# The first part's order of work with additions to its ranks, a buffer of its own for the second chunk's q, and x in a pool of its own

## The chip, the cores and the metric

The kernel runs on one core of a Trainium2 chip. The core has five engines that run side by side, each working through its own instructions in the order in which they were written: TensorE (PE, matrix products and transposes into PSUM), VectorE (DVE), ScalarE (ACT), GpSimd (POOL, used only for constants at the start) and SyncE (SP, which here does nothing but issue DMA transfers). An instruction waits for semaphores that others raise; while it waits, everything behind it on its engine waits too. The metric is the device time of one execution, in microseconds (us).

## The reference

Pooled attention, then a feed-forward layer with softplus. Cut to what is computed:

```python
# q, k, v: 8 batches x 8 heads x 576 positions x 64
k_p = k.reshape(B, H, 72, 8, D).mean(axis=3)      # 72 pooled keys
v_p = v.reshape(B, H, 72, 8, D).mean(axis=3)
scores = (q @ k_p^T) / sqrt(D);  attn = softmax(scores)
x = (attn @ v_p) as 4608 tokens x 512
h = x @ w_in                                      # 512 x 2048
g = max(h, 0) + log1p(exp(-|h|))                  # softplus
out = g @ w_out                                   # 2048 x 512
```

## The kernel before, in words

The 4608 tokens are cut into 18 chunks of 256 (two tiles of 128). For each chunk the kernel makes the attention (transposes of q, scores, minimum, exponentials, sum, division, transposes of the probabilities, product with the pooled values, which gives x), then the products with w_in, softplus, and the products with w_out. x, the weights and g are each split into a rounded high part and a low rest, and three products (high by high, high by low, low by high) stand for one.

There are two parts, each with an order of its own, which a planner writes. This case is mostly about the first part: chunks 0 to 2 complete, the attention of chunk 3, and, at the same time, the loading and conversion of the weights. The weights come in as 64-bit floats; for each of 16 blocks (128 columns of w_in and 128 rows of w_out) DVE takes six instructions and ACT one to build a 32-bit number and split it (lines 791 to 822: `bits`, `clamp`, `shift`, `sign`, `lowest`, `high` on ACT, `rest`). Chunks 0 to 2 use each block as soon as it is converted, which gives PE work while the next block is converted. The second part (chunks 3 to 17) starts when the first part's products end, at about 200 us of the trace, and uses from chunk 4 on a scheme with fewer products, for which combined weights were made and put to memory (`t_dram`), and are loaded back by `load_sums`.

**The planner** (`Order`). The kernel first lists its operations with `op(engine, cost, fn, after, slots, ...)`: on which engine, how long it is thought to take, which operations it follows, and which buffers ("slots") it takes. An operation's rank is the longest chain of planned costs behind it; `first` is added to it. `run` then goes through time: of the operations that can start on the engine that is next to be ready, within 0.4 us of its earliest start, the one with the highest rank plus `first` is taken. The outcome is the order of the instructions of each engine, and the buffer of each slot:

```python
t, o = max(((t, o) for t, o in could if o.engine == best[1] and t < min(best[0], by)),
           key=lambda x: (x[1].rank + x[1].first - ..., -x[1].i))
```

The planner's times order the work; on the chip each engine follows that order and waits where it must. Operations are numbered as they are listed: 0 to 21 are batch 0 of keys and values, 22 to 39 batch 1, then ten for each of the weight blocks 0 to 10 (40 to 49 for block 0, the first two being loads on SP, and so on), seventeen for each of the blocks 11 to 15, then the attention of chunks 0, 1 and 2, the products of chunks 0 and 1 (five operations for each of 16 blocks), the attention of chunk 3, the products of chunk 2, and the keys of batch 2.

**SP's queue at the start.** All loads are issued by SP, in the planned order. They are: batch 0's two key halves and its leftover rows (`kvst` L867, `kvl` L855), chunk 0's q (L308), the first half of weight block 0 (`wst` L760), chunk 1's q, the second half of block 0 (L757), batch 1's first key half, batch 0's two value halves, batch 1's second key half and leftover rows, chunk 2's q, block 1, chunk 3's q, and so on.

**The buffer of q.** One buffer holds the q of a chunk (tag `A4`). In the first part chunks 1 and 2 use the buffer of chunk 0, so a tile of q is loaded only when PE has transposed the same tile of the chunk before (`q_free`, set by the operation `qT`, L337):

```python
if 0 < c < N1:
    qt_[c] = qt_[0]
...
o_q.append(op(SYNC, 1.4, load,
              [] if c == 0 else [q_free[c - 1, t]] if c < N1 else ...
```

**The staging slots.** Four slots of 4 KB a partition (kind `ld`: tags L, X4, X5, X6) hold the key and value halves and the leftover rows until PE has used them (`kps` L921, `vps` L938, `kvlp` L880), and later the raw blocks 11 to 15 of the weights. Batch 0's values have a place of their own.

**Other buffers.** `spin` rotates the tags of the transposed q (`qT`), of the outputs (`o`) and of a conversion buffer (`wg`) in the order in which the instructions are written. x has two buffers (`X01`, `X23`) in the pool `one`; the minima and sums (`mn`, `sm`) have a pool of two buffers each behind it; `pe` is a tile with 16 floats more than it uses.

## Time and profile before

| | |
|---|---|
| three runs | 916.7, 917.85, 921.63 us; median 917.85 |
| the profiled execution | 915.2 us |
| its span, first to last instruction | 913.5 us |
| mean granted TensorE clock | 0.994 |
| PE, busy with products | 888.3 us, 97% of the span |
| DVE, ACT | 648.7 us (71%), 407.3 us (45%) |
| moved by DMA | 191.12 MB, mean 209 GB/s |

The span is the time from the first to the last instruction of the profiled execution; its own time is 1.7 us longer, and the median of the runs 2.65 us longer still. In the rows of stages that follow, the columns are: the stretch in us, its length, then for PE, PE's weight loads, DVE, ACT and POOL the busy us with the number of instructions, then the granted PE clock (1.00 is full speed), the mean busy share of the 16 DMA engines (which can pass 1, since packets overlap) and GB/s. In rows of a timeline the columns are start and length, both in us, engine, line, operation, the tile written and the tiles read, shapes and count, and in brackets the idle time just before with what ended it. Rows of waits give who waited, for whom, the total in us, how often, and the longest.

### The profile page before, as it was taken

Reading aid. Unit: us, or ns where it says so; the run is one execution under the profiler, and the core shown is the slowest. Engines: PE = TensorE matmul, PEld = TensorE weight load, DVE = VectorE, ACT = ScalarE, POOL = GpSimd, SP = SyncE. Lnnn points to the kernel's source line nnn. Section 1 sums busy time; section 2 is a strip of 40 time slices with the busy share of each in tenths; the row PEclk is TensorE's granted clock in tenths of the full one; section 3 lists DMA queues with packets and bytes.
Section 4 is the critical chain, followed back from the end, with each engine's and each line's share of the span. In section 5 each row is a group of like instructions: output and inputs, shape, how many; then the busy total and the mean of one; then the engine's idle time right before and its main releaser. Section 6 shows DMA issues by size and latency. Waiting matters only on the chain.

```text
span 913.5 us, 20504 instructions
## 1 busy us (share of the span) xinstructions
PE 888.3 (97%) x8304; PEld 842.9 (92%) x8304; DVE 648.7 (71%) x1600; ACT 407.3 (45%) x824; POOL 2.4 (0%) x19
## 2 busy tenths in 40 slices
PE   4899999999999999999999999999999999999997
PEld 2678989888899999999999999999999999999997
DVE  4799988867877767787777755787666565747454
ACT  4765433344354544444353535453535343434332
POOL 1000000000000000000000000000000000000000
PEclk9899999999999999999999999999999999999999
DMA  8974625545789679789868866687656565746572
GB/s 234 265 255 144 211 93 187 153 158 155 261 288 270 215 208 249 222 256 238 236 208 243 245 201 198 215 252 223 222 168 222 192 208 184 230 144 233 161 238 84
DMA packets 107085, 191.12 MB, mean 209 GB/s; under 512 B 46064, under 2 KB 60400, under 8 KB 106992
## 3 DMA queue, kind: packets, MB, share of 16 engines
q1 hardware_dynamic: 106992, 189.82, 68.0%
q8 instruction: 65, 1.06, 0.5%
q14 instruction: 28, 0.23, 0.1%
HBM read 167.25 MB, written 22.54 MB: 208 GB/s over the span
## 4 chain that ended last, share of the span: by engine, by line
PE 94%; DVE 3%; DMA 1%; ACT 0%; issue 0%; SPq 0%; DVEq 0%; ACTq 0%
PE h L494 43%; PE m L684 30%; PE acc L516 7%; PE sc L357 3%; PE acc L576 3%; PE avp L461 2%; PE qTp L337 2%; PE avp L468 1%; PE ptp L420 1%; PE ltp L432 1%; DMA kvst<-in_k_dram 1%; PE kps L921 1%; DMA kvl<-in_v_dram 1%; DVE pm L397 0%; PE kvlp L880 0%
## 5 line engine op out<-in xcount | busy, mean ns | idle before, releaser
L494 PE MATMUL h<-x,w 128*128 128x256 f32 x3456 | 430.2, 279 | 0.7 <-DVE w L822 0.7
L494 PEld LDWEIGHTS h<-x,w 128*128 128x128 f32 x3456 | 414.9, 188 | 4.1 <-DVE w L822 0.9
L543 ACT ACTIVATE g<-h 128x512 f32<-128x512 f32 x120 | 71.8, 598 | 279.3 <-PE h L494 278.7
L684 PE MATMUL m<-w,so 128*128 128x256 f32 x1344 | 172.6, 278 | 0.0
L684 PEld LDWEIGHTS m<-w,so 128*128 128x128 f32 x1344 | 162.6, 188 | 0.0
L684 PE MATMUL m<-w,gh 128*128 128x256 f32 x672 | 131.9, 285 | 0.0
L594 DVE TENSOR_TENSOR sf<-g 128x128 f32<-128x128 f32 x112 | 32.8, 293 | 130.3 <-ACT g L543 129.4
L684 PEld LDWEIGHTS m<-w,gh 128*128 128x128 f32 x672 | 101.9, 188 | 1.9
L608 ACT CAST so<-sf 128x512 fp32r<-128x512 f32 x112 | 69.7, 622 | 55.4 <-DVE sf L597 54.9
L684 PE MATMUL m<-w,gl 128*128 128x256 f32 x336 | 93.7, 279 | 0.0
L613 DVE TENSOR_TENSOR so<-sf,so 128x512 fp32r<-128x512 f32 x112 | 77.4, 691 | 21.9 <-ACT so L608 21.7
L564 DVE TENSOR_TENSOR gl<-g,gh 128x384 fp32r<-128x384 f32 (+1 forms) x120 | 67.3, 561 | 0.6 <-ACT gh L557 0.5
L684 PEld LDWEIGHTS m<-w,gl 128*128 128x128 f32 x336 | 63.1, 188 | 0.0
L516 PE MATMUL acc<-w,g 128*128 128x512 f32 x192 | 60.8, 397 | 0.5 <-ACT g L499 0.5
L557 ACT ACTIVATE gh<-h 128x384 fp32r<-128x384 f32 (+1 forms) x120 | 59.2, 493 | 0.0
L499 ACT ACTIVATE g<-h 128x256 fp32r<-128x256 f32 x96 | 31.7, 382 | 59.0 <-PE h L494 52.8
L705 DVE TENSOR_TENSOR o<-o,m 128x256 f32<-128x256 f32 x98 | 39.7, 418 | 3.4 <-ACT o L697 0.6
L516 PEld LDWEIGHTS acc<-w,g 128*128 128x128 f32 x192 | 33.9, 187 | 6.9 <-ACT g L499 0.7
L364 DVE TENSOR_REDUCE mn<-sc 128x4 f32<-128x288 f32 x72 | 31.2, 452 | 10.6 <-PE sc L357 10.4
L516 PE MATMUL acc<-w,gl 128*128 128x512 f32 x96 | 38.0, 396 | 0.0
L597 DVE TENSOR_TENSOR sf<-g,sf 128x128 f32<-128x128 f32 x112 | 32.7, 292 | 3.9
L406 DVE TENSOR_TENSOR pe<-E,sm 128x96 f32<-128x96 f32 x72 | 15.2, 253 | 25.8 <-PE ltp L432 25.8
(165 smaller groups left out, 930.3 us busy)
## 6 DMA issues: line engine op xcount, KB each, us to landing
w<-wi SPq DMA_DIRECT2D x224, 512.0 KB
out_dram<-o SPq DMA_DIRECT2D x36, 256.0 KB
q<-in_q_dram SPq DMA_DIRECT2D x32, 256.0 KB
wst<-in_moe_w_in_dram SPq DMA_DIRECT2D x32, 256.0 KB
wst<-in_moe_w_out_dram SPq DMA_DIRECT2D x16, 512.0 KB
wi<-w SPq DMA_DIRECT2D x16, 512.0 KB
kst<-in_k_dram SPq DMA_DIRECT2D x24, 288.0 KB
vst<-in_v_dram SPq DMA_DIRECT2D x24, 256.0 KB
```

The source lines that it names most:

```text
L494: nc.tensor.matmul(out=ps[:, 0:CT], lhsT=row(w, kc), rhs=x[:, kc], start=first and kc == j == 0, stop=last and kc == KC - 1 and j == 2)
L499: nc.scalar.activation(out=g, in_=ps[:, 0:CT], func=AF.Softplus)
L516: nc.tensor.matmul(out=accs[c][t], lhsT=a[:, ts], rhs=w, start=f == 0 and j == 0, stop=f == FC - 1 and j == 2)
L543: nc.scalar.activation(out=g, in_=x.rearrange("p (b i) -> p b i", i=P), func=AF.Softplus)
L557: nc.scalar.activation(out=gh, in_=quarters(c, x.rearrange("p (b i) -> p b i", i=P)), func=AF.Softplus)
L564: nc.vector.tensor_tensor(out=gl, in0=quarters(c, g), in1=gh.bitcast(F32), op=ALU.subtract)
L594: tt(out=sf[:, 2], in0=g[:, 0], in1=g[:, 2], op=ALU.add)
L597: tt(out=sf[:, 3], in0=g[:, 3], in1=sf[:, 1], op=ALU.subtract)
L608: nc.scalar.copy(out=so[:, 0], in_=ss[c, u])
L613: nc.vector.tensor_tensor(out=so[:, 1], in0=sf, in1=so[:, 0].bitcast(F32), op=ALU.subtract)
L684: nc.tensor.matmul(out=ms[c][n], lhsT=x, rhs=y, start=u == 0 and j == 0 and n in (1, 6, 5, 4), stop=u == FP - 1 and j == 2 and n in (2, 7, ...
L705: nc.vector.tensor_tensor(out=o, in0=in0, in1=m[n], op=how)
```

## The change

1. Chunk 1's q gets memory of its own: a staging slot of the kind `ld`, taken from its load to its second transpose. Its load follows no other operation. Chunk 2's q goes to chunk 0's buffer and follows chunk 0's transposes; chunk 3's is as before.
2. 110 of the first part's 647 operations get an addition to `first`, from -450 to +1090 (the table `HASTE`), by their number.
3. The planner's idea of the first part is altered: loads of weights, keys and values cost 1.5 in place of 1.75; SP begins at 0.8; the table of the exponential is taken to be loaded already.
4. The rotating tags are replaced by the tags that the planner gave the slot (`qT`, `o`, `wg`, `mn`, `sm`).
5. x gets a pool of its own ahead of `one`, with the minima's 64 bytes ahead of it, so that its address modulo 256 is what it was; the sums get a pool behind `one`; `pe` loses its 16 floats.
6. A buffer is made by whichever of its operations comes first in the order (`if not kp`, `if not vp`).
7. In the second part `load_sums` loses its lead of 500.

The second part's list is otherwise unchanged, but it starts from the first part's ends and buffer names.

```diff
+    mpool = ctx.enter_context(tc.tile_pool(name="mpool", bufs=1))
+    xpool = ctx.enter_context(tc.tile_pool(name="xpool", bufs=1))
     one = ctx.enter_context(tc.tile_pool(name="one", bufs=1))
-    two = ctx.enter_context(tc.tile_pool(name="two", bufs=2))
+    spool = ctx.enter_context(tc.tile_pool(name="spool", bufs=1))
...
-    def spin(tags, shape, dtype, name):
-
-        tags.append(tags.pop(0))
-        return one.tile(shape, dtype, tag=tags[-1], name=name)
...
-            x = one.tile([P, 2, HP, CT], F32R, tag={"a": "X01", "b": "X23"}[name or "ab"[c % N1]],
+            x = xpool.tile([P, 2, HP, CT], F32R, tag={"a": "X01", "b": "X23"}[name or "ab"[c % N1]],
...
-        def qT_out(self, ps):
-            self.q = spin(Q, [P, HP, P], F32, "qT")
+        def qT_out(self, ps, tag):
+            self.q = one.tile([P, HP, P], F32, tag=tag, name="qT")
...
-                self.mn = two.tile([P, 2, HP], F32, tag="mn", name="mn")
+                self.mn = mpool.tile([P, 2, HP], F32, tag="mn" + tag, name="mn")
...
-            pe = one.tile([P, 6 * R + 16], F32, tag="pe", name="pe")
-            self.pe = pe[:, 0:6 * R].rearrange("p (a n r) -> p a n r", a=2, n=3)
+            self.pe = one.tile([P, 2, 3, R], F32, tag="pe", name="pe")
...
+    todo.begin, todo.table = {SYNC: 0.8}, "exp"
...
-            return op(SYNC, 1.75, fn, slots=[stages[0 if early else i]], lag=2.2)
+            return op(SYNC, 1.5, fn, slots=[stages[0 if early else i]], lag=2.2)
...
-        o_k = [op(SYNC, 1.75, load(k, i), slots=[st[i]], lag=2.2) for i in range(2)]
-        o_v = [op(SYNC, 1.75, load(v, i), slots=[vt[i] or vt[0]], lag=2.2) for i in range(2)]
+        o_k = [op(SYNC, 1.5, load(k, i), slots=[st[i]], lag=2.2) for i in range(2)]
+        o_v = [op(SYNC, 1.5, load(v, i), slots=[vt[i] or vt[0]], lag=2.2) for i in range(2)]
...
-        o_q, subs = [], []
+        o_q, subs, s_q1 = [], [], Slot("ld")
         for t in range(T):
             def load(t=t):
-                if 0 < c < N1:
+                if c == 1 and c not in qt_:
+                    qt_[c] = one.tile([P, T, H, D], F32, tag=s_q1.name, name="q")
+                elif c == 2:
                     qt_[c] = qt_[0]
                 elif c not in qt_:
                     new_q(c)
                 load_q_tile(c, t)
             o_q.append(op(SYNC, 1.4, load,
-                          [] if c == 0 else [q_free[c - 1, t]] if c < N1 else
-                          [q_free[c - 1, i] for i in range(T)], lag=2.4))
+                          [] if c < 2 else [q_free[0, t]] if c < N1 else
+                          [q_free[c - 1, i] for i in range(T)], [s_q1] if c == 1 else [], lag=2.4))
...
+    HASTE = {27: -130, 29: -3, 34: -120, 36: -120, 45: 40, 46: 20, 48: -180, 55: -2, 56: -10,
+             57: -450, 58: 20, 62: -10, 64: 200, 72: -4, 73: -10, 77: -50, 82: -20, 93: 80, 94:
...
+             220: 40, 222: 5, 230: 2, 231: 70, 255: -20, 258: -10, 259: 40, 274: -180, 283:
+             1090, 285: -50, 286: 230, 289: -10, 295: -10, 297: 670, 302: 50, 308: -4, 316: -10,
+             321: -50, 322: -3, 325: -440, 330: -100, 352: -3, 361: -120, 362: -6, 368: -330,
...
+             575: -140, 583: 30, 610: -20, 620: 4, 635: -80, 638: -310, 641: 40}
+    for i, x in HASTE.items():
+        todo.ops[i].first += x
     with tc.manual_schedule(engines={ACT, DVE, PE, SYNC}):
         for o in todo.run():
             o.fn()
...
         t_ready.setdefault(u, []).append(
             op(SYNC, 2.0, lambda: load_t(u, part), [*after, made[u, part] if u >= U1 else None],
-               lag=2.4, first=500))
+               lag=2.4))
```

More of the change, by code (lines that the diff above doesn't have):

```diff
@@ L251, in k_pool @@
         def k_pool(i):
-            if i == 0:
+            if not kp:
                 kp.append(one.tile([SP, H, D], F32, tag="kp", name="kp"))
@@ L262, in v_pool @@
         def v_pool(i):
-            if i == 0:
+            if not vp:
                 vp.append(one.tile([P, HP, D], F32, tag="vp", name="vp"))
@@ L375, in less, with exp_sum @@
                     [P, 2, 2, SP]), op=ALU.subtract)
-        def exp_sum(self, j, ps):
+        def exp_sum(self, j, ps, tag):
             if j == 0:
-                self.sm = two.tile([P, H], F32, tag="sm", name="sm")
+                self.sm = spool.tile([P, H], F32, tag="sm" + tag, name="sm")
             for m in range(HP):
@@ L384, in exp_sum, with sum @@
                                      accum_out=self.sm[:, h:h + 1])
-        def sum(self):
-            self.sm = two.tile([P, H], F32, tag="sm", name="sm")
+        def sum(self, tag):
+            self.sm = spool.tile([P, H], F32, tag="sm" + tag, name="sm")
             nc.vector.tensor_reduce(out=self.sm, in_=e_[self.c][:, self.t], axis=AX.X, op=ALU.add)
@@ L517, in ffn2, with copy_out @@
                                  start=f == 0 and j == 0, stop=f == FC - 1 and j == 2)
-    def copy_out(c, t, tag=None):
-        o = one.tile([P, DM], F32, tag=tag, name="o") if tag else spin(O, [P, DM], F32, "o")
+    def copy_out(c, t, tag):
+        o = one.tile([P, DM], F32, tag=tag, name="o")
         if t % 2 == 0:
@@ L788, in bits @@
             else:
-                g = x["g", k] = spin(O, [P, 1, 4 * P], I32, "wg")
+                g = x["g", k] = one.tile([P, 1, 4 * P], I32, tag=gslot[k].name, name="wg")
                 up = x["raw", k].unsqueeze(1).rearrange("p x (n w) -> p x n w", w=2)[:, :, :, 1]
@@ L972, in attend @@
             o = op(PE, 0.5, lambda x=x, s=s_q: x.qT(bank(s, "qTp")),
-                   [o_q[t], *([av[c - 1]] if c == N1 else [])], [s_q])
+                   [o_q[t], *([av[c - 1]] if c == N1 else [])], [s_q, *([s_q1] if c == 1 else [])])
             q_free[c, t] = o
-            o = op(ACT, act(512), lambda x=x, s=s_q: x.qT_out(s.tile), [o], [s_q, s_qT])
+            o = op(ACT, act(512), lambda x=x, s=s_q, n=s_qT: x.qT_out(s.tile, n.name), [o], [s_q, s_qT])
             ends, ss = [], [Slot("bank"), Slot("bank")]
@@ L980, in attend, with exp_sum @@
             for i, s in enumerate(ss):
-                d = op(DVE, 0.46, lambda x=x, i=i, s=s: x.least(i, s.tile), [p, *ends],
+                d = op(DVE, 0.46, lambda x=x, i=i, s=s, n=s_mn: x.least(i, s.tile, n.name), [p, *ends],
                        [s, s_mn])
                 if c < N1:
-                    def exp_sum(x=x, i=i, s=s, e=s_E[0], t=t):
+                    def exp_sum(x=x, i=i, s=s, e=s_E[0], t=t, n=s_sm):
                         if c == 0 and 0 not in e_:
@@ L1005, in attend @@
             if c == N1:
-                ends = [op(DVE, 0.75, x.sum, [ex], [s_sm])]
+                ends = [op(DVE, 0.75, lambda x=x, n=s_sm: x.sum(n.name), [ex], [s_sm])]
             o = op(DVE, 1.45, x.norm, ends, [*s_E, s_sm, s_pm, s_pe])
@@ L1054, in feed, with copy @@
                 h = {}
-                def copy(t=t, h=h):
-                    h["o"] = copy_out(c, t)
+                def copy(t=t, h=h, s=s):
+                    h["o"] = copy_out(c, t, s.name)
                 o = op(DVE if t % 2 else ACT, 0.65, copy, [before2], [s, acc_slots[c][t]])
@@ L1142, in pooled_attention_softplus_ffn @@
     other = [b for b in BANKS if b not in acc_banks]
-    kinds = {"h": other[:2], "acc": other[2:4], "bank": other[4:], "ld": LD, "q": "a", "pT": "a", "qT": "ab", "lt_": "a",
+    kinds = {"h": other[:2], "acc": other[2:4], "bank": other[4:], "ld": LD, "q": "a", "pT": "a", "qT": Q, "lt_": "a",
              "pe": "a", "mn": "ab", "sm": "ab", "E": "a", "kp": "a", "vp": "a", "S": "ab", "x": "b",
@@ L1175, in steady_attention @@
             qT_done[c].append(o)
-            o = op(ACT, act(512), lambda x=x, s=s: x.qT_out(s.tile), [o], [s, s_qT])
+            o = op(ACT, act(512), lambda x=x, s=s, n=s_qT: x.qT_out(s.tile, n.name),
+                   [o], [s, s_qT])
             last, ss = [], [Slot("bank"), Slot("bank")]
@@ L1181, in steady_attention @@
             for i, s in enumerate(ss):
-                last = [op(DVE, 0.46, lambda x=x, i=i, s=s: x.least(i, s.tile), [p, *last],
+                last = [op(DVE, 0.46, lambda x=x, i=i, s=s, n=s_mn: x.least(i, s.tile, n.name), [p, *last],
                            [s, s_mn])]
@@ L1198, in probabilities @@
             s_sm, s_pm, s_pe = Slot("sm"), Slot("G"), Slot("pe")
-            o = op(DVE, 0.76, x.sum, [ex], [s_E, s_sm])
+            o = op(DVE, 0.76, lambda x=x, n=s_sm: x.sum(n.name), [ex], [s_E, s_sm])
             o = op(DVE, 0.38, x.reciprocal, [o], [s_sm])
```

6 lines of the change are left out of this document (3 added, 3 removed), and 7 rows, old and new, of the table HASTE.

## The prediction

> **What bounds the kernel now.** I read the page's totals first, then a table of stages, then the waits of TensorE (PE) and of the DMA queue, and last single instructions of the first 50 us.
>
> ```profile
> PE 888.3 (97%) x8304; PEld 842.9 (92%) x8304; DVE 648.7 (71%) x1600; ACT 407.3 (45%) x824; POOL 2.4 (0%) x19
> ```
>
> PE works 888.3 of the 913.5 us, so no new order of the same work can win more than 25.2 us plus what a low clock costs. Where these lie is seen in the table of stages (busy us of each engine with its instructions, granted clock, DMA share, GB/s):
>
> ```profile
> 0.00:18.00 18.00, 8.15 (x90) 4.15 (x90) 6.03 (x11) 7.74 (x30) 2.37 (x19) 1.00 0.84 200
> 18.00:26.00 8.00, 5.29 (x73) 3.31 (x74) 3.76 (x9) 2.52 (x13) 0.00 (x0) 0.57 1.16 294
> 26.00:35.00 9.00, 7.87 (x68) 5.90 (x68) 7.12 (x15) 6.72 (x32) 0.00 (x0) 1.00 0.73 189
> 35.00:40.00 5.00, 4.05 (x77) 3.16 (x81) 4.33 (x9) 4.81 (x22) 0.00 (x0) 0.66 1.10 317
> 40.00:80.00 40.00, 35.01 (x355) 29.70 (x345) 37.03 (x76) 26.32 (x69) 0.00 (x0) 1.00 0.70 230
> 80.00:140.00 60.00, 60.00 (x386) 54.16 (x387) 55.10 (x82) 22.24 (x52) 0.00 (x0) 1.00 0.50 164
> 140.00:200.00 60.00, 59.46 (x393) 52.63 (x392) 47.64 (x104) 23.56 (x60) 0.00 (x0) 1.00 0.51 157
> 200.00:300.00 100.00, 99.76 (x939) 92.41 (x939) 77.65 (x181) 46.72 (x83) 0.00 (x0) 1.00 0.76 238
> 300.00:900.00 600.00, 600.00 (x5872) 589.02 (x5871) 403.67 (x1099) 264.11 (x467) 0.00 (x0) 1.00 0.71 215
> 900.00:913.50 13.50, 8.69 (x76) 8.49 (x74) 6.37 (x16) 2.60 (x5) 0.00 (x0) 0.97 0.10 39
> ```
>
> PE idles 9.85 us before 18, 2.71 to 26, 1.13 to 35, 0.95 to 40 and 4.99 from 40 to 80; then it is full until 900 (0.8 us missing in all), and the last 13.5 us belong to the second part. So what is won before 80 reaches the end one for one, and behind 80 there is nothing to win. From 40 to 80 VectorE (DVE) is the tighter engine, 37.03 of 40 against PE's 35.01. Who PE waits for between 10 and 80 (us in total, times, longest):
>
> ```profile
> PE ltp L432 <- DVE pe L406: 4.9, 4, 1.5
> PE kps L921 <- DMA kvst<-in_k_dram: 3.7, 1, 3.7
> PE sc L357 <- ACT kT L225: 1.6, 2, 1.4
> PE qTp L337 <- DMA q<-in_q_dram: 1.5, 2, 1.2
> PE h L494 <- DVE w L822: 0.7, 1, 0.7
> ```
>
> Two are loads (5.2 us, both before 21 us), three are the order of DVE's and ScalarE's (ACT's) work (7.2 us, all behind 32 us).
>
> **The change part by part.**
>
> *Chunk 1's q in memory of its own.* Now its load waits for chunk 0's transposes, and everything behind it in SP's queue waits too. SP's timeline (start, length), its wait, the chain's piece for the second batch's keys, and DMA microsecond by microsecond:
>
> ```profile
> 6.15 1.75 SPq L760 DMA_DIRECT2D wst<-in_moe_w_in_dram  x2
> 12.07 1.11 SPq L308 DMA_DIRECT2D q<-in_q_dram  x2
> 13.24 0.88 SPq L757 DMA_DIRECT2D wst<-in_moe_w_out_dram  x1
> 14.16 0.42 SPq L867 DMA_DIRECT2D kvst<-in_k_dram  x1
> 15.79 1.15 SPq L867 DMA_DIRECT2D kvst<-in_k_dram  x1
> ```
> ```profile
> SPq L308 <- PE kT L219: 3.2, 1, 3.2
> ```
> ```profile
> 14.16 6.41 DMA kvst<-in_k_dram
> ```
> ```profile
> 10.00:11.00 1.00, 1.00 (x3) 0.29 (x2) 0.77 (x2) 0.00 (x0) 0.00 (x0) 1.00 0.88 279
> 11.00:12.00 1.00, 1.00 (x7) 0.79 (x7) 0.60 (x1) 0.58 (x1) 0.00 (x0) 1.00 0.02 6
> 12.00:13.00 1.00, 0.79 (x9) 0.55 (x8) 0.00 (x0) 0.92 (x3) 0.00 (x0) 1.00 0.00 0
> 13.00:14.00 1.00, 0.97 (x60) 0.97 (x64) 0.20 (x1) 0.97 (x3) 0.00 (x0) 1.00 0.70 160
> ```
>
> SP issues nothing from 7.90 to 12.07, 4.17 us. Without the wait all issues behind it come 4.17 us sooner: chunk 1's two q transfers at 7.9, w_out of block 0 at about 9.1, the second batch's first keys at 10.0. The transfers themselves gain less, since the DMA engines are busy to 11.0 with what is there already; the hole that is filled is 0.98 + 1.00 + 0.30 = 2.3 us. So keys that land at 20.57 land at about 18.3, and PE's 3.7 us wait for them shrinks by 2.3. Bounds: 0, if another load is put ahead of the keys in the hole, and 4.17, if the keys pass some of what is ahead. I take 2.3. PE's 1.5 us for q (the two waits before 17 us) need no term of their own: they lie ahead of the same keys.
>
> The price is a staging slot. Four exist; batch 0's two key halves and its leftover rows take three, and the fourth, which batch 1's first keys had, may now go to q. Those keys then need one that is given back, when these end:
>
> ```profile
> 5.97 1.08 PE L921 MATMUL kps<-kvst,zm 128*64 128x256 f32 x2 [5.97 <-DVE kvst L914]
> 10.10 1.11 PE L921 MATMUL kps<-kvst,zm 128*64 128x256 f32 x2
> 16.42 0.63 PE L337 MATMUL qTp<-ident,q 128*128 128x128 f32 x4 [0.33 <-DMA q<-in_q_dram]
> ```
>
> The first is free at 7.05, before SP comes to the keys at 10.0: no cost. The second key half, issued at 15.79 now and at 11.6 then, would take the one free at 11.21: no cost. If they were given the slots the other way round, 1.2 us of the 2.3 would go. q's own slot is free at 17.05 or sooner, for the second batch's values, which come later.
>
> *Clock.* While PE waits for these keys its clock falls. Timeline of PE, then the clock (the column after the engines) by microsecond:
>
> ```profile
> 20.70 3.65 PE L921 MATMUL kps<-kvst,zm 128*64 128x256 f32 x8 [3.66 <-DMA kvst<-in_k_dram]
> 35.95 1.11 PE L357 MATMUL sc<-kT,qT 64*64 64x72 f32 x27 [1.37 <-ACT kT L225]
> 42.27 0.39 PE L432 MATMUL ltp<-ident,pe 128*96 128x128 f32 x2 [1.20 <-DVE pe L406]
> 51.01 0.39 PE L432 MATMUL ltp<-ident,pe 128*96 128x128 f32 x2 [1.44 <-DVE pe L406]
> ```
> ```profile
> 18.00:19.00 1.00, 0.00 (x0) 0.00 (x0) 0.00 (x0) 1.00 (x9) 0.00 (x0) 0.76 1.03 354
> ...
> 25.00:26.00 1.00, 1.00 (x53) 0.92 (x46) 0.46 (x1) 0.00 (x0) 0.00 (x0) 0.83 1.32 173
> ...
> 38.00:39.00 1.00, 1.00 (x12) 0.24 (x5) 1.00 (x2) 1.00 (x9) 0.00 (x0) 0.50 1.07 351
> ```
>
> The clock falls in the microsecond from 18 and is back within that from 25; from 20.70 to about 25.3 PE runs at half speed, which costs 2.3 us; from 35.95 to 39.0 again, 1.5 us. With the keys at 18.3 the idle is 1.3 us instead of 3.66. Rows disagree on whether that is short enough: after 1.20 and 1.44 us the clock stayed (it is 1.00 from 40 to 80), after 1.37 us at 35.95 it had fallen. So 0 to 3.8 us, and I take 1.1, half of the first stretch.
>
> The Trainium skill, "TensorE: Matmul & The Clock Gate", Part 1, says that the clock halves after an idle window of about 3.4 us and recovers after one that is busy, and that the windows run free of the kernel. By that no idle of 1.3 us can halve it, and 2.3 would stand where I have 1.1; the fall before 35.95, with no idle there above 1.4 us, speaks against the rule taken alone, so I keep the half.
>
> *The list's corrections.* 110 of the 647 operations of the first part get an addition to their rank. By the planner's costs in the code, ranks run from 0 to about 165 in this stretch, so the entries beyond 100 decide an order wherever two operations of an engine are ready within 0.4 us, and those below 10 settle near ties. No instruction is added. Early entries push batch 1's leftover products (27), second key half (34) and key transposes (36) back by 120 to 130 on PE, draw forward one exponential of chunk 1 (283), its rounded x (297) and its transposed weights (286) on ACT, and push the conversion of weight blocks 0 and 1 back where attention is ready (48, 57). They concern just the 7.2 us of PE's waits for DVE and ACT. Both ends: all 7.2 won, or as much lost again. DVE limits it: it must deliver the same work, and from 40 to 80 it has 40 - 37.03 = 3.0 us to spare. Earlier it idles more (4.2 us from 18 to 26, 1.9 to 35), in part for a transfer that now starts sooner:
>
> ```profile
> DVE wg L791 <- DMA wst<-in_moe_w_out_dram: 2.8, 1, 2.8
> ```
>
> I take 2.5, a little below DVE's 3.0. Behind 80 PE has no idle, so the many later entries are worth 0; cover there is PE's backlog of products, and without it each would cost what it displaces.
>
> *Edits at nothing.* The planner's own costs (1.5 for 1.75, a start at 0.8, the table already there) act through the order alone and are in the 2.5. Fixed tags in place of rotated ones give the planned buffers. Moving x, mn and sm adds no instruction, and x keeps its phase; tiles ahead of pe move by 64 bytes modulo 256, for which no row shows a price: 0. In the second part the load of the combined weights loses its lead of 500; PE misses only 0.24 us from 200 to 300, and the cover is the time from the last of these issues to the products of the block that it serves. The issues' first and last start, and the products of chunk 4, 48 of this kind for eight blocks:
>
> ```profile
> L665 SPq DMA_DIRECT2D w<-t x16: 370/444/857, 222.0 to 259.9; - x16
> ```
> ```profile
> L684 PE MATMUL m<-w,gh x40: 276/280/385, 261.7 to 299.8; 128*128 128x256 f32 x40
> ```
>
> The last block's products come near 299, 39 us after its load at 259.9. I take 0; a load that came later than that would cost what it is late.
>
> *Sum.* 2.3 + 1.1 + 2.5 = 5.9 us. The profiled execution took 915.2 us (913.5 us of span and 1.7 around it), so 909.3; the median of the three runs, 917.85, lies 2.65 above that execution, so the forecast as a median is 912.0.
>
> **The rivals.**
>
> *Corrections that work fully.* Hole 2.3, clock 2.3, and 6 of the 7.2: 10.6 us, 907.3. For it: the waits are in four or five places with neighbours ready. Against: DVE's 3.0 us.
>
> *Hidden by DVE.* Keys come sooner, but DVE sets when the first products can run, and the 2.3 us turn into longer waits for pe and w; only some 1 us stays: 916.9. For it: DVE's 93% from 40 to 80 and the four waits for pe. Against: DVE too starts sooner, since its own 2.8 us wait is behind the same stall.
>
> *Slower: batch 1's keys come too late.* Ranks cut by 120 to 130 hold them back on PE, whose order is fixed once written. Then kT, for which PE waits 1.6 us already, is later than now, chunk 2's scores with it, and the DVE results behind them. Decisive is whether kT is ready later than the 36 us of now; then the waits for kT and pe double (+1.6 + 4.9) with another cold stretch like the second (+1.5), against 2.3 won: +5.7, 923.5. For it: the size of the entries. Against: the work put ahead on PE is ready and short.
>
> *The stall only changes its owner.* q has the slot, and the keys wait for one in its place, as long as q did: 917.9. The slot free at 7.05 speaks against it.
>
> **How the numbers follow.** The forecast has 0.50, working fully 0.16, hidden by DVE 0.20, slower 0.09, changed owner 0.05. The forecast's own range is 908.5 to 915.0 (0 to 2.3 for the clock, 0 to 4 for the ranks and the hole's 1.2 for a slot). A measurement of this kernel can tell about 0.5%, 4.6 us, from no change: faster is below 913.3. Of the forecast's 0.50 about 0.36 lie there, with 0.16 of the first rival 0.52; same has 0.14, 0.20, 0.05 and 0.01, together 0.40; slower 0.08. From 906.5 to 919.0 hold nearly all of the forecast, hidden and changed owner, and half of working fully: about 0.82.
>
> **What would show it.** SP issues chunk 1's q within 0.2 us of the weights before it, and DMA has no empty microsecond between 11 and 14; PE's wait for the keys is about 1.3 us and they land near 18.3; the clock at 20 to 25 is 1.00 or 0.50; PE's waits for pe, kT and w add up to about 4.7; PE is full from about 75 on and the second part begins some 6 us sooner, at 194 instead of 200. The forecast is wrong if DMA has a new hole before the keys, if kT comes later than 36 us, if DVE's idle before 35 stays as it is, or if PE shows idle between 80 and 300.

## The result, and the profile after

The changed kernel takes 905.18 us in the median of four runs (902.67 to 906.46), beside 919.74 us for the kernel before on the same chip: a ratio of 0.9844, 95% interval 0.9813 to 0.9875. In a second set of six runs it was 0.9876 (0.9847 to 0.9906). The forecast was 912.0 with a range of 906.5 to 919.0. The direction is right, but the time lies below the range: the gain is 14.6 us (11.4 by the second ratio), where the sum had 5.9. The profile of the kernel after shows the fastest of these ten executions (902.67 us); the second set has a profile of its own (906.36 us), and where they differ in what is read from them, it is said.

The totals of the kernel after, then its stages in the columns used before:

```profile
PE 884.9 (98%) x8304; PEld 840.5 (93%) x8304; DVE 649.3 (72%) x1600; ACT 407.4 (45%) x824; POOL 2.4 (0%) x19
```
```profile
0.00:18.00 18.00, 8.89 (x93) 4.57 (x94) 8.43 (x15) 8.28 (x37) 2.37 (x19) 1.00 0.82 236
18.00:26.00 8.00, 7.32 (x120) 5.90 (x119) 7.65 (x18) 7.63 (x29) 0.00 (x0) 1.00 1.09 316
26.00:35.00 9.00, 8.52 (x114) 5.61 (x112) 7.43 (x20) 7.79 (x33) 0.00 (x0) 1.00 0.95 268
35.00:40.00 5.00, 4.66 (x49) 4.09 (x48) 4.45 (x11) 4.95 (x25) 0.00 (x0) 1.00 1.05 384
40.00:80.00 40.00, 39.35 (x348) 33.76 (x348) 38.73 (x71) 23.42 (x52) 0.00 (x0) 1.00 0.64 205
...
140.00:200.00 60.00, 60.00 (x460) 53.50 (x459) 49.77 (x109) 24.77 (x58) 0.00 (x0) 1.00 0.48 161
200.00:300.00 100.00, 100.00 (x906) 94.19 (x906) 77.83 (x192) 44.90 (x80) 0.00 (x0) 1.00 0.78 242
```

The span fell from 913.5 to 900.9 us, 12.6. PE's busy time fell by 3.4 (888.3 to 884.9; in this execution no stretch ran at a low clock), its idle time by 9.2. By the rows, idle fell by 0.7 up to 18 us, 2.0 to 26, 0.7 to 35, 0.6 to 40, 4.3 to 80 and 0.8 from 80 to 300. DVE is 2.4 us further on at 18 us (8.43 for 6.03), 6.3 at 26 and 8.4 at 80. PE's largest waits from 10 to 80 us in the kernel after:

```profile
PE qTp L335 <- DMA q<-in_q_dram: 1.7, 1, 1.7
PE kps L918 <- DMA kvst<-in_k_dram: 0.8, 1, 0.8
PE sc L355 <- ACT qT L342: 0.7, 1, 0.7
```

The waits for `pe` (4.9), `kT` (1.6) and the weights (0.7) have all but gone in this execution; in the second profile PE still waits 2.0 us for `pe`. DVE's wait up to 80 us for the scores that PE makes, before and after:

```profile
DVE mn L364 <- PE sc L357: 7.3, 5, 3.0
```
```profile
DVE mn L362 <- PE sc L355: 2.1, 1, 2.1
```

SP's timeline in the kernel after, its wait, and the microsecond in which DMA moves nothing:

```profile
5.99 1.41 SPq L757 DMA_DIRECT2D wst<-in_moe_w_in_dram  x2
7.44 0.47 SPq L754 DMA_DIRECT2D wst<-in_moe_w_out_dram  x1
12.15 0.37 SPq L306 DMA_DIRECT2D q<-in_q_dram  x1
12.56 0.58 SPq L864 DMA_DIRECT2D kvst<-in_k_dram  x1
13.24 1.38 SPq L306 DMA_DIRECT2D q<-in_q_dram  x2
```
```profile
SPq L306 <- PE qTp L335: 5.7, 2, 3.3
```
```profile
12.00:13.00 1.00, 0.85 (x46) 0.74 (x48) 0.00 (x0) 1.00 (x3) 0.00 (x0) 1.00 0.00 0
```

This is not the picture that was forecast. SP still stands still for 4.2 us, from 7.91 to 12.15, and DMA still has its hole. What waits now is the second tile of chunk 2's q (operation 302, with +50), which goes into chunk 0's buffer. What has changed is what stands ahead of the stall: w_out of block 0, at 7.44 instead of 13.24. Batch 1's keys go out at 12.56 instead of 14.16, ahead of chunk 1's q. PE's timeline after shows them in use:

```profile
15.27 0.63 PE L335 MATMUL qTp<-ident,q 128*128 128x128 f32 x4 [1.74 <-DMA q<-in_q_dram]
16.66 1.91 PE L918 MATMUL kps<-kvst,zm 128*64 128x256 f32 x8 [0.76 <-DMA kvst<-in_k_dram]
```

They are worked on at 16.66 instead of 20.70, in 1.91 us instead of 3.65 at half clock. The first products of the kind `acc<-w,gh` on the second part's line start at 192.4 instead of 203.9; from there to the end of the span it is 708.5 us, and 709.6 before. So some 11 us are won in the first part and one behind it.

### The profile page after: what moved, and what is told of

It reads as the page before. It is cut to its first block, busy times and chain, and to the rows that moved or that the text cites. A ratio compares the mean times of both kernels' runs of the same rounds, so it can differ in the third digit from the quotient of the medians.

```text
span 900.9 us, 20496 instructions
## 1 busy us (share of the span) xinstructions
PE 884.9 (98%) x8304; PEld 840.5 (93%) x8304; DVE 649.3 (72%) x1600; ACT 407.4 (45%) x824; POOL 2.4 (0%) x19
## 4 chain that ended last, share of the span: by engine, by line
PE 96%; DVE 1%; DMA 1%; ACT 1%; issue 0%; SPq 0%; DVEq 0%; ACTq 0%
PE h L490 45%; PE m L680 30%; PE acc L512 7%; PE acc L572 3%; PE sc L355 2%; PE avp L457 2%; PE qTp L335 2%; PE ptp L416 2%; PE avp L464 1%; PE ltp L428 1%; PE kps L918 1%; DMA kvl<-in_v_dram 1%; DMA kvst<-in_k_dram 0%; ACT E L380 0%; PE kvlp L877 0%; DVE o L701 0%
```

## The experiments

Ratios are to the kernel before on the same chip, with 95% intervals. Operation numbers are those of the planner's list.

### The forecast's first term: q's own memory alone

```diff
-                if 0 < c < N1:
+                if c == 1 and c not in qt_:
+                    qt_[c] = one.tile([P, T, H, D], F32, tag="L", name="q")
+                elif c == 1:
+                    pass
+                elif c == 2:
                     qt_[c] = qt_[0]
...
+        todo.ops[24].slots[0].name, todo.ops[25].slots[0].name = "X4", "L"
```

The last line gives slot X4 to batch 1's second key half and slot L to its first value half, which thus follows q there.

> The kernel before, every engine's order as it was, with one edit: chunk 1's q lies in the staging slot that batch 0's first key half gives back at about 7 us, so SP no longer waits for chunk 0's transposes at 7.9 us. This is the forecast's first term by itself. The forecast expects the DMA hole from 11 to 13.3 us filled, the keys at about 18.3, 2.3 us won and 0 to 2.3 for the clock, ratio to before 0.995 to 0.9975. Theory C (DVE's early start counts too): block 0's second half also lands about 4 us sooner, DVE's wait of 2.8 us near 19 us goes, and 4 to 7 us are won, ratio 0.992 to 0.995.

Measured: 0.9973 (0.9948 to 0.9998), 2.5 us. SP and PE's waits from 10 to 80 us in this kernel:

```profile
6.13 1.74 SPq L760 DMA_DIRECT2D wst<-in_moe_w_in_dram  x2
7.99 1.36 SPq L308 DMA_DIRECT2D q<-in_q_dram  x2
9.39 2.09 SPq L757 DMA_DIRECT2D wst<-in_moe_w_out_dram  x1
11.53 0.43 SPq L867 DMA_DIRECT2D kvst<-in_k_dram  x1
```
```profile
PE ltp L432 <- DVE pe L406: 5.2, 4, 1.6
PE sc L357 <- ACT qT L344: 1.9, 1, 1.9
PE sc L357 <- ACT kT L225: 1.4, 1, 1.4
PE kps L921 <- DMA kvst<-in_k_dram: 1.0, 1, 1.0
```

This is the forecast's mechanism by itself: no stall, and PE's wait for the keys is 1.0 us (forecast 1.3, before 3.7). The waits for `pe` and `kT` stay, and one of 1.9 us for `qT` is new. The forecast had 2.3 for the hole and 1.1 for the clock that follows from it; the run measures both together, and its interval, 0.2 to 4.8 us, does not tell the two apart. The mean granted clock of its twelve executions is 0.997, that of the kernel before beside them 0.995. The profile is of the slowest of the twelve (918.05 us, median 914.42), so its rows show how the loads go, not what is won.

The same loads can be had without a buffer, by putting w_out of block 0 (operation 41) and batch 1's keys (23) ahead of the q that stalls:

```diff
+        order = todo.run()
+        at = order.index(todo.ops[268])
+        for n in (23, 41):
+            order.remove(todo.ops[n])
+            order.insert(at, todo.ops[n])
```

> The kernel before, with two loads moved in SP's queue and nothing else: the second half of weight block 0 and batch 1's first key half stand ahead of chunk 1's stalled q instead of behind it. No rank is corrected and q is shared. Theory A: the keys come sooner but the waits for pe, kT and w take the place of the wait removed; at most 2.3 us, about 917.4. Theory B: the wait of 3.7 us for the keys and both cold stretches (2.3 and 1.5 us) go, 5 to 7 us, about 913.5.

Measured: 0.9967 (0.9939 to 0.9996), 3.0 us, between its two theories. The stall of q stays in SP's queue, and as far as the intervals tell the gain is the same: what counts is that the keys and w_out are not behind it.

### The clock alone

24 extra products of the identity, whose results are overwritten, stand ahead of chunk 1's second q transposes.

```diff
+            if (self.c, self.t) == (1, 1):
+                for _ in range(24):
+                    nc.tensor.matmul(out=ps[:, 0:P], lhsT=ident, rhs=ident, start=True, stop=True)
```

> The kernel before, with 24 more products of the identity with itself on PE just ahead of the last transposes of chunk 1's q (written over by these), in time in which PE waits for the keys; nothing else differs. They are to keep the clock up. Both theories: if the clock alone counts, PE's eight key products last about 1.9 us instead of 3.65, the stretch from 20.7 to 25.3 shrinks by about 2.3 us and the time falls to about 917.4; if what follows waits for something else anyway, the time stays at 919.7. The wait for the keys, by their landing at 20.57, does not move.

Measured: 1.0034 (1.0007 to 1.0060). Stages of this kernel, and the extra products in PE's timeline:

```profile
18.00:26.00 8.00, 8.00 (x118) 6.72 (x117) 4.44 (x11) 4.03 (x23) 0.00 (x0) 1.00 1.08 300
26.00:35.00 9.00, 7.51 (x64) 5.57 (x62) 6.79 (x15) 6.40 (x29) 0.00 (x0) 1.00 0.86 222
35.00:40.00 5.00, 3.70 (x88) 2.87 (x88) 4.77 (x12) 5.00 (x23) 0.00 (x0) 1.00 1.07 314
```
```profile
16.22 5.52 PE L339 MATMUL qTp<-ident 128*128 128x128 f32 x48
```

In this profile the clock is 1.00 where it was 0.57 and 0.66, and PE idles 1.3 us in 35 to 40 (0.95 before) and 1.5 in 26 to 35 (1.1). But the run does not price the clock. The extra products last 5.5 us and fill more than the wait: the keys' products start at 22.11 instead of 20.70 and, though twice as fast, end at 24.05 instead of 24.35. And the profile is one of just two of the ten executions with a mean clock of 0.999 (914.53 and 913.47 us); the other eight have 0.994 to 0.997 and take 918.95 to 921.96 us, so the edit does not keep the clock up.

What the clock is worth is seen in the kernel before itself, of which 102 executions ran beside these experiments. The 22 with a mean clock of 0.997 or more have a median of 914.0 us, the 22 with 0.992 or less one of 920.1. Part of that may be idle time that makes the clock fall. In the two profiles of the kernel after idle time is not the difference: PE idles 16.0 and 16.6 us in all, while its busy time is 884.9 and 888.1 us and the span 900.9 and 904.7, with mean clocks of 0.999 and 0.995.

### The corrections

First the kernel after without any addition to the ranks (the loop over `HASTE` left out), then the kernel after with all of them but chunk 1's q in chunk 0's buffer as before:

> The changed kernel with no addition to any rank; chunk 1's q keeps its own memory, the planner's new costs, fixed tags and pools stay. Theory A (the gain is the corrections' order of PE, DVE and ACT): own memory alone gives what was forecast for the hole and half a cold stretch, 2.3 + 1.1 = 3.4 us, about 916.3 against 919.7 before. Theory B (half of the gain is that batch 1's keys land about 4 us sooner and PE's clock never falls, which any order of loads with that effect gives): PE's wait for the keys falls from 3.7 us to under 1, the clock stays at 1.00 until 40 us, together 6 to 7 us, about 913; the waits for pe, kT and w stay near 7 us in total.

> The changed kernel with all 110 additions, but chunk 1's q in chunk 0's buffer as before, so that its load again waits for chunk 0's transposes. Theory A: most of the 14.5 us stays, at least 10, about 909 or less, since the order on PE, DVE and ACT is what counts. Theory B: the keys are issued behind the stalled q again, land near 20 us, the clock falls, and about 6 us of the gain go, 911 to 914.

Measured: 0.9926 (0.9903 to 0.9949) and 0.9927 (0.9903 to 0.9952), against 0.9844 and 0.9876 for the whole. Without corrections SP does not stand still in the first 23 us, and still 40 to 80 us holds waits of PE:

```profile
PE ltp L428 <- DVE pe L402: 3.4, 3, 1.5
PE sc L355 <- ACT qT L342: 2.5, 2, 2.0
PE sc L355 <- ACT kT L223: 1.4, 1, 1.4
```

So the corrections are worth 0.5 to 0.8%, 4.6 to 7.5 us, though they bring the stall back. Without them 6.8 us are left. That is theory B's number, but 3.7 of it can come from the places of the tiles (below), which neither theory had. With q shared 6.7 us are left too, so some 5 to 8 of the gain go, near theory B's 6. q's own memory, taken away last, is worth as much as the corrections; alone it was worth 2.5. The pieces of this change depend on one another. With 33 of the 110, those whose operation is planned before 60 us:

```diff
     for i, x in HASTE.items():
+        if i not in EARLY_ONES:
+            continue
```

> The changed kernel with the 33 additions whose operations stand before 60 us in its list, the other 77 dropped. The forecast's step 'behind 80 PE has no idle, so the later entries are worth 0' expects the changed kernel's ratio to before within 0.3%, about 0.984 to 0.987. The other view, that the later entries keep the engines in step, expects new idle of PE between 60 and 200 us and 2 us or more lost, ratio 0.988 or above.

> The changed kernel with the 33 early additions alone, once more, on one chip with the changed kernel. If the 77 later entries are worth what the trace of the first run showed behind 80 us (0.7 us of PE's idle), the ratio lies within 0.002 of the changed kernel's; if they are worth the 4 us between the medians, it is 0.004 or more above it.

> The changed kernel, unaltered, beside the other runs on one chip. Ratio to before 0.981 to 0.988, as measured first.

Measured: 0.9910 (0.9875 to 0.9946), and beside the whole change on one chip 0.9919 (0.9890 to 0.9949) against 0.9876: 909.07 against 905.64 us. By the medians the early ones alone are worth about 1 us over none (0.9926), within the intervals, and the other 77, which the forecast put at 0, 3.4. PE's idle time over the whole span, span less busy time, divides otherwise: 22.2 us without corrections, 17.9 and 18.3 in the two profiles with the early ones, 16.0 and 16.6 with all. By that the early ones save about 4 us and the later ones about 2. The medians also hold what the clock did: its mean was 0.999 without corrections and 0.996 to 0.997 with the early ones. So both groups are worth something, and how much each is stays open.

The profiles with the early ones and with all, taken side by side, differ by 1.5 us at the second part's first `acc<-w,gh` (197.7 and 196.2) and by 2.7 behind it. One place behind it is seen. PE and DVE in the kernel with q's own memory alone, where the wait is longest:

```profile
297.48 1.59 PE L357 MATMUL sc<-kT,qT 64*64 64x72 f32 x32 [3.99 <-DVE E L371]
```
```profile
286.36 1.15 DVE L212 TENSOR_TENSOR vst<-vst 128x512 f32<-128x512 f32 x2 [3.22 <-DMA vst<-in_v_dram]
...
292.39 1.15 DVE L212 TENSOR_TENSOR vst<-vst 128x512 f32<-128x512 f32 x2 [4.56 <-DMA vst<-in_v_dram]
```

DVE stands in its order at value halves that have not landed, the subtraction behind it is late, and PE's scores wait for a bank: 4.0 us here, 1.1 without corrections and in one of the two profiles with the early ones, nothing in the other, in either profile of the whole change, and in the one of before. So one kernel can have this wait in one execution and not in the next. The second part's list is planned from where the first ends, so corrections in the first part move this too. The first of these value loads goes out like this with the early corrections (the profile with the wait), then with all:

```profile
272.92 1.25 SPq L258 DMA_DIRECT2D vst<-in_v_dram  x2
```
```profile
265.59 1.27 SPq L258 DMA_DIRECT2D vst<-in_v_dram  x2
```

### The order of three loads

In the kernel after: batch 1's keys further forward (on SP ahead of the stalled q 302, on PE ahead of operation 310); w_out of block 0 held back behind chunk 1's q, as before (five moves, written here as a loop); batch 1's keys held back behind chunk 1's q.

```diff
+        for n, before in ((23, 302), (33, 310)):
+            order.remove(todo.ops[n])
+            order.insert(order.index(todo.ops[before]), todo.ops[n])
```
```diff
+        for n in (302, 23, 268, 269, 41):
+            order.remove(todo.ops[n])
+            order.insert(order.index(todo.ops[42]), todo.ops[n])
```
```diff
+        order.remove(todo.ops[23])
+        order.insert(order.index(todo.ops[269]) + 1, todo.ops[23])
```

> The changed kernel with batch 1's first key half put ahead of chunk 2's stalled q in SP's queue, and the products that use it put ahead of that q's transposes on PE; nothing else is moved. If the loads still set the start, PE's two waits of 1.7 us (q) and 0.8 us (keys) shrink to under 1 us together and the kernel gains 1.5 to 2.5 us on the changed one, ratio to before about 0.982. If DVE and ACT set the pace from 14 us on, the same idle comes back a few us later as waits for their results, and the ratio stays at 0.984 to 0.986.

> The changed kernel with the second half of weight block 0 put behind chunk 1's q in SP's queue, as in the kernel before; the orders of PE, DVE and ACT are those of the changed kernel. Theory C (the gain is that DVE, the tighter engine, starts on block 0 about 6 us sooner, which fills its idle before 35 us): DVE waits 3 to 5 us for this load near 14 us, and 4 us or more of the gain go, ratio 0.988 or above. Theory B (batch 1's keys and the clock): the keys land no later, at most 1.5 us go, ratio 0.984 to 0.986.

> The changed kernel with batch 1's first key half put behind chunk 2's and chunk 1's q in SP's queue; the orders of PE, DVE and ACT are those of the changed kernel. The keys are issued about 2 us later. Theory B: PE waits 2 to 4 us more for them, its clock may fall, and 3 to 5 us of the gain go, ratio 0.988 to 0.990. Theory C: DVE has block 0 to work on meanwhile and what is late is made up before 80 us; at most 1.5 us go, ratio 0.984 to 0.986.

Measured, on one chip: 0.9856 (0.9826 to 0.9887), 904.99 us; 0.9922 (0.9894 to 0.9950), 911.39; 0.9897 (0.9866 to 0.9928), 908.25. Waits with block 0 late, then with the keys late:

```profile
DVE wg L788 <- DMA wst<-in_moe_w_out_dram: 6.3, 1, 6.3
```
```profile
PE kps L918 <- DMA kvst<-in_k_dram: 4.2, 1, 4.2
```

Against the 905.0 of the first, w_out ahead of q is worth 6.4 us and the keys 3.3; keys that come sooner still are worth nothing. So theory C holds for block 0 and theory B for the keys. The kernel after itself did not run on this chip; by its own two ratios the two are worth 4.2 to 7.2 and 1.9 to 4.9 us. Both held-back kernels also have long stretches at a low clock (0.68 from 26 to 35 us with block 0 late, 0.66 from 18 to 26 with the keys late), so a slower PE is in these prices. The price of block 0 belongs to the order of the kernel after: in the order of before w_out goes out just as early with the two loads moved (7.98 us) and DVE no longer waits for it, and the whole gain there is 3.0 us. The forecast had no term for DVE's start on block 0.

### What was counted at nothing: the planner's numbers and the places

The planner's numbers alone in the kernel before, then the places alone:

```diff
+    todo.begin, todo.table = {SYNC: 0.8}, "exp"
...
-            return op(SYNC, 1.75, fn, slots=[stages[0 if early else i]], lag=2.2)
+            return op(SYNC, 1.5, fn, slots=[stages[0 if early else i]], lag=2.2)
...
```

> The kernel before with only the planner's own numbers changed: 1.5 in place of 1.75 for three kinds of loads, SP's start at 0.8, and the exponential's table taken as loaded at the start. Nothing else of the change. The list without corrections stood at 0.9926 and chunk 1's q in its own memory alone at 0.9973; 4.3 us between the two belong to the planner's numbers, to the places of tiles or to the fixed tags. If the planner's numbers make them: about 0.995 (4 us), w_out of block 0 and batch 1's first keys ahead of chunk 1's q on SP, TensorE's wait for the keys gone or under 1.5 us, and its waits for pe below the 5.2 us of the run with q's own memory. If places or tags make them: 0.999 to 1.001, with the order on SP and TensorE as in the kernel before.

```diff
+    mpool = ctx.enter_context(tc.tile_pool(name="mpool", bufs=2))
+    xpool = ctx.enter_context(tc.tile_pool(name="xpool", bufs=1))
     one = ctx.enter_context(tc.tile_pool(name="one", bufs=1))
...
-            pe = one.tile([P, 6 * R + 16], F32, tag="pe", name="pe")
+            self.pe = one.tile([P, 2, 3, R], F32, tag="pe", name="pe")
```

> The kernel before with only the places of the kernel after: mn and x in pools of their own ahead of the others, sm behind, pe without its padding, so that all tiles of the large pool begin at 0 modulo 256 where those ahead of pe began at 192. The order stays. If places are worth 0 as forecast: 0.999 to 1.001. If part of the unexplained 4.3 us comes from them: about 0.996, and TensorE's mean per product from 310 to 880 falls below 124.2 ns for h<-x,w and 128.4 ns for m<-w,so of before.

Measured: the numbers alone make it slower, 1.0062 (1.0042 to 1.0082), against the expectation: the loads at the top keep their order, and PE idles 0.7 us from 80 to 140 and 1.9 from 140 to 200. In all it idles just 1.0 us more than before, but is busy for 893.7 us instead of 888.3, with a clock of 0.92 from 40 to 80; why the clock falls there was not followed further. The places alone make it faster, 0.9960 (0.9938 to 0.9981), 3.7 us, with the same order of instructions and nearly the same mean clock (0.995 and 0.994). The first 18 us with q's own memory alone (staging tiles at 192 modulo 256, as before), then with the places alone (at 0):

```profile
0.00:18.00 18.00, 9.86 (x95) 5.64 (x96) 6.98 (x13) 7.13 (x25) 2.36 (x19) 1.00 1.02 258
```
```profile
0.00:18.00 18.00, 9.14 (x90) 5.10 (x90) 6.09 (x12) 7.83 (x30) 2.36 (x19) 1.00 0.74 212
```

GB/s for one unit of DMA share are 253 and 286; the kernel before has 238 (200 at 0.84), the kernel after 288 (236 at 0.82). The products' time hardly moves (128.4 to 128.2 ns for one `m<-w,so`), nor does the busy time of DVE (648.7 to 648.2 us) or ACT (407.3 to 407.0). The loads into the staging tiles got cheaper, and what waits for them waits less with the places alone:

```profile
PE kps L922 <- DMA kvst<-in_k_dram: 3.0, 1, 3.0
```

That was 3.7, and DVE's wait for w_out of block 0 falls from 2.8 to 1.6 us. That these waits make the whole 3.7 us of the median is not shown.

The places alone and q's memory alone multiply to 0.9933, and all but the corrections gave 0.9926: in company the planner's numbers, with the tags and the lead that goes, cost nothing.

### 64 bytes more: weights and moving operand

In the kernel after, 64 unused bytes ahead of x (x and all behind it at 64 modulo 256, weights at 192); the same bytes behind x; the weights at 128 and x at 0; weights 0 and x 64; weights 0 and x 0. The last three are made by moving pools, and the constants and the minima's buffer move along. The `w` tiles hold 32-bit floats, not the bfloat16 that one expectation names.

```diff
+    mpool.tile([P, 16], F32, tag="pad", name="pad")
     xpool = ctx.enter_context(tc.tile_pool(name="xpool", bufs=1))
```

> The changed kernel with 64 bytes of padding ahead of x, so that x and all tiles behind it lie 64 bytes later modulo 256; the order is the same. The forecast gave a shift of 64 bytes no price, so the ratio should be the changed kernel's within 0.002. If the place of x modulo 256 counts, PE's mean of 279 to 280 ns for a product of h, or ACT's and DVE's means for x and g, change, and the ratio with them.

> The kernel after with 64 unused bytes behind x instead of ahead of it: x of the first chunks stays at 0 modulo 256, everything behind it (so, gh, gl, E, qT, pT and x of the last chunk) moves to 64. The run with x moved too took 15.5 us more. If each product pays for its own moving operand: h<-x,w stays near 124.0 ns in the first part, m<-w,so goes to about 132 ns and m<-w,gh to about 199 ns, half of the loss, ratio about 0.996 (913 to 914 us). If x alone carried the loss: 0.988 (905 to 906). If the place of the other tiles carried it: 1.004 (921).

> The kernel after with the weights' pool ahead of the constants: the bfloat16 weights begin at 128 modulo 256 instead of 192, x and all others stay. If the distance between weights and moving operand decides (128 bytes here as in the run with x moved by 64): about 1.004, h<-x,w near 126.5 ns. If the moving operand's own place decides: 0.988, 124.0 ns. A gain below 0.986 would mean that the weights' place has a price of its own.

> The kernel after with the weights' pool at 0 modulo 256 and x and all other tiles at 64: the distance from weights to moving operand is 64 as in the kernel after, but both stand elsewhere. If the distance decides a product's time: h<-x,w near 124.0 ns and m<-w,so near 128.2 ns, and only the loads pay for their tiles at 64, which was 0.4% between the kernel before and the one with its places changed: ratio about 0.991 (909). If x has to stand at 0 or the weights at 192: 126 ns or more and about 1.004 (921).

> The kernel after with everything at 0 modulo 256: weights, x and the other tiles, distance 0, and the weights' transfers begin at 0 too. If only the distance of 128 is bad: 0.984 to 0.988 (902 to 906), with h<-x,w at 124.0 ns or below. If 64 is the one good distance: h<-x,w at 126 ns or more, ratio 1.000 to 1.004. The loads' GB/s for each unit of DMA share in the first 18 us should be 284 to 293 in both cases, as in every kernel with its staging tiles at 0.

Products from 310 to 880 us, grouped by line and shape (count, then busy us, mean ns of one), of the kernel after and of the five in the same order:

```profile
L490 PE MATMUL h<-x,w 128*128 128x256 f32 x2323 | 288.1, 279 | 0.0
L680 PE MATMUL m<-w,so 128*128 128x256 f32 x1159 | 148.6, 277 | 0.0
```
```profile
L491 PE MATMUL h<-x,w 128*128 128x256 f32 x2256 | 285.4, 282 | 0.0
L681 PE MATMUL m<-w,so 128*128 128x256 f32 x1140 | 150.6, 281 | 0.0
```
```profile
L492 PE MATMUL h<-x,w 128*128 128x256 f32 x2270 | 285.1, 280 | 0.0
L682 PE MATMUL m<-w,so 128*128 128x256 f32 x1139 | 150.7, 281 | 0.0
```
```profile
L490 PE MATMUL h<-x,w 128*128 128x256 f32 x2267 | 286.9, 282 | 0.0
```
```profile
L491 PE MATMUL h<-x,w 128*128 128x256 f32 x2318 | 287.8, 279 | 0.0
```
```profile
L491 PE MATMUL h<-x,w 128*128 128x256 f32 x2245 | 287.1, 284 | 0.0
```

Products overlap, so the rate is busy time over count:

| weights, x (modulo 256) | distance | one h<-x,w | ratio (95%) | median us |
|---|---|---|---|---|
| 192, 0 (after) | 64 | 124.0 ns | 0.9876 (0.9847 to 0.9906) | 905.64 |
| 192, 64 | 128 | 126.5 | 1.0042 (1.0023 to 1.0061) | 921.12 |
| 192, 0; the rest 64 | 64; 128 | 125.6 | 1.0020 (1.0001 to 1.0039) | 918.72 |
| 128, 0 | 128 | 126.6 | 1.0034 (1.0013 to 1.0054) | 919.84 |
| 0, 64 | 64 | 124.2 | 0.9887 (0.9862 to 0.9911) | 907.51 |
| 0, 0 | 0 | 127.9 | 1.0079 (1.0052 to 1.0106) | 925.32 |

In `h<-x,w` the tile of weights is the one that stands still and x moves through; in `m<-w,so` it is the other way round, and `so` lies with "the rest". With all tiles but the weights kept together, the rate goes with the distance and not with where either stands: 64 bytes is the good one of three, 128 costs 2% of a product, 0 costs 3%. `m<-w,so` does the same: 128.2 ns in the kernel after, 132.1 and 132.3 in the second and third rows. But a product's own two tiles are not all that counts. In the third row the x of these products, chunks 4 and later, still lies at 0, 64 bytes from the weights (only chunk 2's x lies at 64, and its products are over by then), and yet one `h<-x,w` takes 125.6 ns instead of 124.0. So of the 2.5 ns between the first two rows 1.6 come with the place of the other tiles: that each product pays for its own moving operand alone, as one expectation had it, is not so, and the cause is open. In the fifth row the loads go to tiles at 64: 260 GB/s for a unit of DMA share (208 at 0.80), at a ratio 0.001 above that of the kernel after, inside the intervals; whether the loads' places are worth as much there as the 3.7 us in the order of before stays open. No version beat the kernel after clearly: keys first is within its interval.

## Why the prediction was right or wrong

*The first term, 2.3 for the hole.* In the order of before the mechanism holds: without the stall PE's wait for the keys fell to 1.0 us, and the median by 2.5 (0.2 to 4.8), the clock included. In the kernel after it does not happen, since the stall and the hole stay; that the term fits the time there is luck.

*Wrong, though half named as a rival at 0.05: the stall only changes its owner.* It did, and SP's issue within 0.2 us of the weights did not come. But the rival's new owner was the keys, waiting for a slot, at a price of nothing won (917.9). The owner is chunk 2's q, and w_out passes the stall, which in this order is worth more (6.4 us) than the stall is long (4.2). The operations concerned could have been followed through the list.

*Wrong: "tiles ahead of pe move by 64 bytes modulo 256, for which no row shows a price: 0".* This step failed outright; it measured 3.7 us (1.7 to 5.7). That no row shows a price is no reason for 0: the bounds should have been open. A row stood in the prediction: the first 18 us move 200 GB/s at a share of 0.84, 238 for a unit, where 40 to 80 us give 329 (with tiles at 0 they give 288, so that half of the gap has another cause). The change kept x's place modulo 256, and the runs show what that was worth: with x and all behind it 64 bytes on, the whole gain is gone (1.0042). The Trainium skill, "DMA: Bandwidth & Descriptors", "How a descriptor splits into AXI transactions", says that a piece which does not start on a 256-byte boundary begins with a transaction from the boundary below and pays for the bytes it does not use. It speaks of what a transaction reads; here the places written to in SBUF moved. The measured 238 to 260 GB/s for a unit of share with tiles at 192 or 64, and 274 to 293 with tiles at 0, go the same way; that this is the cause inside the DMA engines is not shown by these runs.

*Wrong: "behind 80 PE has no idle, so the many later entries are worth 0".* They measured 3.4 us by the medians and about 2 by PE's idle time. One profiled execution had no wait there; others of nearly the same list wait 1.1 to 4.0 us for late value halves. Of the 4.2 us between the two profiles 1.5 lie ahead of the second part, and their place was not found.

*Wrong cap: DVE's 3.0 us to spare from 40 to 80.* DVE did 8.4 us more by 80 us (4.8 in the second profile), 6.3 of it by 26. The reserve was its idle ahead of 35, which the prediction named and set aside. What fell are above all its waits for scores from PE (7.3 us before, 2.1 after) and for w_out of block 0 (2.8, none after; in the second profile block 1's has 2.3). So the term of 2.5 for the corrections was too small: all of them are worth 4.6 to 7.5 us. That the early ones act on PE's waits fits: they take some 4 us off its idle time.

*The planner's numbers, "in the 2.5".* Alone they cost 5.7 us, with the rest nothing: a planner's input has no price of its own, only the list that results.

*The clock, 1.1.* No run prices it by itself. Profile against profile 3.4 us of busy time went, but the second profile of the same kernel has a cold stretch again, with 888.1 us busy. Over all executions the mean clock rose from 0.9945 to 0.9972; with PE busy nearly all the time, that share of 915 us is an estimated 2.5 us. By this the term had the right sign and was too small, and it is part of the pieces below, not one beside them.

*The slower rival* had a direction wrong. Entries that hold batch 1's later keys back let chunks 0 and 1 pass; PE's wait for `kT` became 0.2 us, where doubling was feared. *Hidden by DVE* fell with the cap. *Corrections that work fully* came nearest in time (907.3); that is luck as far as its hole and its clock go, and the places were no part of it. The forecast's own range does not follow from its terms either: 0 to 2.3 for the clock, 0 to 4 for the ranks and 1.1 to 2.3 for the hole span 909.2 to 916.8 around the median of 917.85, not 908.5 to 915.0.

Measured pieces: 2.5 for q's memory, 3.7 for the places, 0.6 for all else without corrections (0.9933 to 0.9926), about 1 for the early and 3.4 for the later corrections, 11.2 in all, against 11.4 (0.9876 of 917.2) for the whole. The last three are differences between neighbours, so that the sum has to close; the one finding in it is that q's memory and the places together (0.9933) give what all but the corrections give (0.9926).

## What to carry to other kernels

An edit that moves tiles is not free until a row says so: look at the addresses modulo 256, at GB/s for a unit of DMA share, and at busy time over count of the products. A stall in a queue costs what stands behind it, so ask which load stands there, not how long the stall is. An engine's reserve is counted over all the time ahead of the bottleneck, not in the stage where it is tight; and one profiled execution that shows no wait late in a kernel does not show that the order there is worth nothing.

## What the runs showed of the hardware

Two findings were not expected. The first is the rate of loads into tiles at 0 modulo 256, given above. The second is that a product's time depends on the distance between the weights and the other tiles, modulo 256: 124.0 ns at 64 bytes, 126.5 at 128, 127.9 at 0, which over the kernel is 15 to 19 us of 905 (ratios of 1.0042 and 1.0079 for 0.9876). It is not the product's own two tiles alone (125.6 ns in the third row). Why is open, and other distances were not tried.

Cold stretches differ between executions of one kernel. The second profile of the kernel after, beside the 1.00 of the first, and PE's timeline just ahead of the fall:

```profile
35.00:40.00 5.00, 4.22 (x46) 3.48 (x48) 4.81 (x10) 2.81 (x15) 0.00 (x0) 0.60 0.97 312
```
```profile
35.78 0.43 PE L428 MATMUL ltp<-ident,pe 128*96 128x128 f32 x2 [2.03 <-DVE pe L402]
```

The Trainium skill, "TensorE: Matmul & The Clock Gate", Part 1, says that the clock's windows run free of the kernel. These two executions do not test that: the one with the fall idles 2.03 us just ahead of it, and the other does not.
